# Which queue issues the first loads of an adaLN transformer block: the conditioning vector, two x blocks and a piece of w_mod

## The chip, the cores and the metric

The kernel runs on one core of a Trainium2 chip. The metric is the device time of one execution in microseconds (us), the median over several executions; lower is better. The engines of the core are named as in the profile: PE (matrix products; PEld is its loading of stationary operands), DVE (vector), ACT (scalar, activations), POOL (general), and SP, which here only issues transfers. ACT issues transfers too; a q behind a name (SPq, ACTq) marks the issuing instructions.

## The reference

One block of a transformer with adaptive layer norm, for 2048 rows of width 640, in bfloat16. The conditioning vector `c` yields six rows of modulation, which enter both layer norms and both residual additions:

```python
mod = (silu(c) @ w_mod).reshape(1, 6, 1, -1)          # w_mod: 640 x 3840
sa, ca, ga, sb, cb, gb = (mod[:, i] for i in range(6))
h = layernorm(x) * (1 + ca) + sa
x = x + ga * A(h)     # attention: 32 heads of 20, causal, window of 256, then @ wo
h = layernorm(x) * (1 + cb) + sb
x = x + gb * B(h)     # (sigmoid(h @ w_gate) * (h @ w_up)) @ w_down, inner width 1536
```

## The kernel before

The rows are worked in eight chunks of 256 rows, each two blocks of 128 rows. For every chunk the kernel normalizes and modulates x, turns it, multiplies by wqkv, turns Q and K, forms the scores, the exponentials and the products with V, multiplies by wo, and runs the gated MLP. PE's order interleaves the stages of neighbouring chunks. The order of all operations is a table, `PRIO`: each of the 2121 operations has one number, whose rank is its place and whose remainder by five is its engine (0 PE, 1 ACT, 2 DVE, 3 POOL, 4 SP). Every engine works through its own list strictly in that order. Where one engine depends on another, it waits for a semaphore; a transfer signals one of 24 semaphores in turn. Before the change, `schedule()` also ran a small model of the times, by which it chose the buffer (slot) of each tile.

The change concerns the first microseconds. What has to arrive there, in the names of the profile:

- `in_c_dram` into a corner of the buffer `oT`: the conditioning vector, 5 rows of 128 values, 1.2 KB.
- `in_A_x_dram` into `x`: the 128-row blocks of the input, 160 KB each. Block 0 goes to buffer x10, block 1 to x11.
- `in_w_mod_dram` into `wd`: the first 1280 columns of w_mod (the shift and scale of the first layer norm), in five pieces of 128 rows, 320 KB each. They lie in the buffer that later holds w_down, so the profile calls them `wd`.
- `in_A_wqkv_dram` into `wqkv`: four pieces of 400 KB (Q and K), one of 800 KB (V).

What is done with them until the first product with wqkv, engine by engine:

- PE runs matmuls without a result (L649, six, later four; L660 between the pieces), a small product that turns `c` into a column (L634), then for each piece of w_mod ten matmuls (L668, `S<-silubc,wd`), and ahead of the last piece the turning of the normalized blocks (L668, `<-ident,x`). Then the products of chunk 0 with wqkv begin (L668, `M<-wqkv,hT`).
- DVE takes the layer-norm statistics of block 0 (L776), then `c_col` (L636), the aggregate of block 0 (L778), the two steps of silu(c) that follow ACT's tanh (L638, L640), and only then the statistics of block 1 (L776, L778). POOL raises both variances to the power -1/2 (L783), DVE normalizes (L796). When PE has turned the blocks and the last piece is in, DVE copies the modulation out of PSUM (`mA`, L761), and DVE and ACT apply it (L847, L846); that gives `hT`.
- ACT issues two transfers, loads its table (L637), and computes the tanh of `c_col` (L637).

Each transfer here is issued by `dma()`, whose issuing line is L570 in the profile.

Of the kernel before, what the change touches and what calls it, by code (L numbers as in the profile page):

```python
# [22 lines left out]
SM_SCALE = 1.0 / math.sqrt(DH)  # L23
VW = 22
NDMA = 24
SWITCH = 0.095
ENGATTR = {"pe": "tensor", "act": "scalar", "dve": "vector", "pool": "gpsimd", "sp": "sync"}
ENGS = ("pe", "act", "dve", "pool", "sp")
OVERLAP = {"pe": 0.0, "act": 0.085, "dve": 0.075, "pool": 0.045, "sp": 0.0}


class Res:
# [49 lines left out]
class Prog:  # L82
# [69 lines left out]
    def schedule(self):  # L152


        free = {e: START for e in ENGS}
        bw = 0.0
        lastturn = False
        order = {e: [] for e in ENGS}
        dmacnt = [0] * NDMA
        dmalast = [None] * NDMA  # L160
        rr = 0
        pemode = 0
        portend = 0.0
        freed = {}

        def slot_time(pool, s):
            ten = pool.tenant[s]
            if ten is None:
                if not all(x.done for x in pool.init[s]):
                    return None  # L170
                return max([x.end + x.lat for x in pool.init[s]], default=0.0)
            return None if ten.left else freed[ten]

        def take(t, s):
            ten = t.pool.tenant[s]
            t.prev = list(t.pool.init[s]) if ten is None else list(ten.rel)
            t.slot = s
            t.pool.tenant[s] = t

        for o in sorted(self.ops, key=lambda x: x.prio):  # L180
            assert all(d.done for d in o.deps), o.tag
            e = ENGS[o.prio % 5]
            assert e in o.engs, (o.tag, e)
            o.eng = e
            st = max([o.tmin, free[e] + (SWITCH if e == "pe" and o.mode != pemode else 0.0)]
                     + [d.end + (0.0 if d.eng == "pe" and e == "pe" else d.lat) for d in o.deps])
            if o.isdma and e == "sp":
                st = max(st, bw - QMAX)
            for t in o.tiles:
                if t.slot is None:  # L190
                    step = 1 if t.mate is None else 2
                    best = None
                    for s in range(0, len(t.pool.tenant), step):
                        rts = [slot_time(t.pool, s + k) for k in range(step)]
                        if None not in rts and (best is None or max(rts) < best[0]):
                            best = (max(rts), s)
                    assert best is not None, (o.tag, t.name)
                    if t.mate is None:
                        take(t, best[1])
                    else:  # L200
                        take(t, best[1] + t.odd)
                        take(t.mate, best[1] + 1 - t.odd)
                for x in t.prev:
                    st = max(st, x.end + x.lat)
            if e == "dve" and o.port:
                st = max(st, free["pool"])
            elif e == "pool":
                st = max(st, portend)
            o.start = st
            if e == "pe":  # L210
                pemode = o.mout
            dur = o.dur[e]
            free[e] = st + dur - OVERLAP[e]
            if e == "dve" and o.port:
                portend = free[e]
            if o.isdma:
                turn = o.dlat > 3.0
                if e == "sp" and bw - st > 2.0:
                    free[e] += 0.35 if o.dur[e] > 1.0 else 0.1
                bw = max(st + o.dlat, bw + (MIXED if turn != lastturn and bw > st + o.dlat else 0.0)) + o.work  # L220
                lastturn = turn
                o.end = max(bw - 0.83, st + dur)
                s = rr
                rr = (rr + 1) % NDMA
                dmacnt[s] += 16
                o.key, o.val = f"d{s}", dmacnt[s]
                if dmalast[s] is not None:
                    o.deps.append(dmalast[s])
                dmalast[s] = o
            else:  # L230
                o.end = st + dur
            order[e].append(o)
            o.done = True
            for t in o.tiles:
                t.left -= 1
                if t.left == 0:
                    last = {}
                    for x in t.ops:
                        if x.isdma:
                            last[x] = x  # L240
                    for e2 in ENGS:
                        xs = [x for x in t.ops if x.eng == e2 and not x.isdma]
                        if xs:
                            last[e2] = max(xs, key=lambda x: x.start)
                    t.rel = list(last.values())
                    freed[t] = max(x.end + x.lat for x in t.rel)
        self.order = order
        self.span = max(o.end for o in self.ops)

    def emit(self):  # L250
        nc = self.nc
# [85 lines left out]
def c_pe(n):  # L337
    return max(n, 64) / 2400.0 + 0.0027


PE_EPS = 0.14
PRIO = [
# [117 lines left out]
]  # L460
TR1 = 2
NPH = 3
NPQ = 2
PQ = ()
KEEP = 3
DSAFE = 1.5
START = 0.8
PORTLAG = 0.05
MIXED = 0.55
NPB = 0  # L470
GB = ()
XT0 = 1
# [9 lines left out]
DEDGE = 0.245  # L482
FILL = 1
WSE = (("dve", "pool"), ("dve", "pool"))
QMAX = 4.5
WDT = 72.0
PAIR = 0
PAIRO = 0
# [5 lines left out]
def build(nc, A_x, A_wqkv, A_wo, B_x, B_w_gate, B_w_up, B_w_down, c, w_mod, out, S=2048):  # L494
# [50 lines left out]
    c_row = p_oT.aps[0][0:NDT, 0, 0:128]  # L545
# [19 lines left out]
    def dma(dst, src, work, reads=(), writes=(), prio=50.0, tmin=0.0, tag="dma", extra=(), nonc=False, hold=(), eng="sp", lat=0.08 + DSAFE, dur=0.5, dlat=2.24):  # L565
        def fn(e, _):
            if nonc:
                with nc.allow_non_contiguous_dma(reason="small"):
                    return e.dma_start(dst(), src())
            return e.dma_start(dst(), src())  # L570
        return A(eng, fn, dur, reads=reads, writes=writes, prio=prio, work=work, tmin=tmin, tag=tag, extra=extra, hold=hold, lat=lat, dlat=dlat)
# [23 lines left out]
    def load_x(pool, b, prio, tmin=0.0, eng="sp", extra=()):  # L595
# [2 lines left out]
            tag=f"x{b}" if pool is p_x0 or b < 2 * KEEP else f"y{b}", eng=eng, lat=(0.6, 0.9)[b] if b < 2 else 0.2 + DSAFE, extra=extra)  # L598
        return t

    dma(lambda: c_row, lambda: c.rearrange("o (t p) -> (o t) p", p=128), 0.05, writes=[R_crow], prio=-1, eng="act", lat=0.3)
    wm_src = w_mod.rearrange("(t p) f -> p t f", p=128)
    Rm = [[R(f"wm{i}_{kt}") for kt in range(NDT)] for i in range(4)]
    wm23 = hhall[:, 0:2 * NDT * D].rearrange("p (t f) -> p t f", t=NDT)
    wm_ap = [wd[:].rearrange("p a b -> p (a b)")[:, 0:6400].rearrange("p (t f) -> p t f", t=NDT),
             wu[:].rearrange("p a b -> p (a b)")[:, 0:6400].rearrange("p (t f) -> p t f", t=NDT),
             wm23[:, :, D:2 * D], wm23[:, :, 0:D]]

    def load_bulk(dst, src, Rs, work, prio, tag, extra=(), cuts=(1, 2, 3, 4, 5), **kw):
        k = 0  # L610
        for m in cuts:
            dma(lambda k=k, m=m: dst[:, k:m, :], lambda k=k, m=m: src[:, k:m, :], work * (m - k), writes=Rs[k:m],
                prio=prio + 0.01 * k, tag=tag, extra=list(extra), **kw)
            k = m
# [6 lines left out]
    x0 = {}  # L621
    keep = {}
    keep[0], keep[1] = load_x(p_x1, 0, 0), load_x(p_x1, 1, 0, eng="act", tmin=1.25)
    load_bulk(wm_ap[0], wm_src[:, :, 0:1280], Rm[0], 0.93, 0.2, "wm0", lat=0.9)
    for i in range(4):
        load_w3(320 * i, 320 * i + 320, 1.1, 0.30 + 0.005 * i, "wq" if i < 2 else "wk", lat=0.5)
    keep[2], keep[3] = load_x(p_x1, 2, 0.32), load_x(p_x1, 3, 0.33)
# [24 lines left out]
    for i in range(5):  # L652
        o = A("pe", warm, 0.85 if i < 4 else 0.43, prio=90, reads=[R_z], extra=wprev, tag="warm", writes=[R("w")])
# [302 lines left out]
    last = {"s": fills, "p": []}  # L956
# [350 lines left out]
```

## Time and profile before

| | |
|---|---|
| median of 3 runs | 325.69 us (325.58 to 326.39) |
| the profiled execution: first to last instruction | 324.3 us |
| PE busy | 317.3 us (98%) |
| PEld busy | 222.7 us (69%) |
| DVE, ACT, POOL busy | 211.8, 212.3, 187.2 us |
| granted TensorE clock | 1.000 |
| read from HBM, written | 21.30 MB, 5.25 MB |

The page gives the profiled execution's span, 324.3 us, and no time around it; the median of the timed runs is 1.4 us longer. Where PE is busy nearly all the time, the reader should not look at shares but at the few places where PE waits, and most of that waiting lies in the first 11 us. The rows of the timeline give a start, a duration, an engine with its line, and in brackets the idle time before it with what ended it.

### The profile page before, as it was taken

What the parts mean: (1) busy time and instruction counts of PE and PEld (TensorE: products, weight loads), DVE (VectorE), ACT (ScalarE), POOL (GpSimd) and SP (SyncE); (2) the same over time, 40 slices, a digit from 0 to 9 for tenths busy, and PEclk for the clock granted to TensorE, in tenths of its full rate; (3) what the DMA queues carried; (4) which work ended last, traced back from release to release, by engine and by line L of the source; (5) the groups of instructions that cost most, each with busy time, mean ns of one, the idle gap of its engine ahead of it and who ended that gap; (6) DMA issues with size and microseconds to landing.
All of it is one profiled execution on the core that took longest, in us unless ns stands there. A gap on an engine that the chain in (4) does not pass through costs nothing.

```text
span 324.3 us, 11594 instructions
## 1 busy us (share of the span) xinstructions
PE 317.3 (98%) x4872; PEld 222.7 (69%) x4873; DVE 211.8 (65%) x424; ACT 212.3 (65%) x316; POOL 187.2 (58%) x276
## 2 busy tenths in 40 slices
PE   8999999989999999999999999999999999999997
PEld 3564545446776568765776467877786788787885
DVE  5797898778687959674477475837463769264332
ACT  1899985889876687788687867786767764011120
POOL 5128869976668694847585939382939691012100
DMA  7998799989891383824405394340213032202101
GB/s 249 371 333 299 165 269 180 200 137 183 260 164 22 83 109 77 152 61 101 85 22 82 97 103 110 92 69 5 81 40 88 3 79 53 76 20 64 40 2 40
DMA packets 71694, 37.85 MB, mean 117 GB/s; under 512 B 45274, under 2 KB 70362, under 8 KB 71642
## 3 DMA queue, kind: packets, MB, share of 16 engines
q1 hardware_dynamic: 69616, 35.31, 48.3%
q10 hardware_dynamic: 2026, 1.80, 2.1%
q8 instruction: 38, 0.62, 0.8%
q14 instruction: 14, 0.11, 0.1%
HBM read 21.30 MB, written 5.25 MB: 82 GB/s over the span
## 4 chain that ended last, share of the span: by engine, by line
PE 73%; DMA 2%; SPq 2%; DVE 1%; POOL 1%; issue 0%; DVEq 0%
PE M L668 61%; PE S L669 6%; PE M L669 5%; DMA gbc<-gate 2%; SPq L803 2%; DVE wd L1192 1%; POOL x L793 0%; POOL st L788 0%; DVE hh L1211 0%; POOL E L1040 0%; DVE x L1230 0%; DVEq L310 0%
## 5 line engine op out<-in xcount | busy, mean ns | idle before, releaser
L1040 POOL TENSOR_SCALAR_AFFINE_SELECT E<-E 128x512 bf16<-128x512 bf16 (+1 forms) x176 | 142.6, 836 | 68.7 <-ACT E L1015 67.0
L1015 ACT ACTIVATE E<-S 128x512 bf16<-128x512 f32 (+2 forms) x184 | 150.9, 878 | 47.4 <-PE S L669 46.5
L668 PE MATMUL M<-wqkv,hT 128*128 128x480 bf16 (+1 forms) x340 | 73.9, 355 | 0.6 <-ACT hT L846 0.5
L668 PE MATMUL M<-h2T,wu 128*128 128x256 bf16 x480 | 68.0, 273 | 0.5 <-DVE hh L1211 0.5
L668 PE MATMUL M<-h2T,wg 128*128 128x256 bf16 x480 | 67.8, 273 | 0.0
L668 PE MATMUL M<-wd,hh 128*128 128x320 bf16 (+2 forms) x396 | 58.1, 295 | 0.0
L1209 ACT ACTIVATE sig<-M 128x512 f32<-128x512 f32 x48 | 28.9, 602 | 44.1 <-PE M L668 41.7
L1211 DVE SCALAR_TENSOR_TENSOR hh<-sig,M 128x512 bf16<-128x512 f32 x48 | 32.4, 681 | 37.1 <-ACT sig L1209 24.0
L668 PEld LDWEIGHTS M<-h2T,wu 128*128 128x128 bf16 x480 | 45.9, 98 | 8.4 <-issue 1.2
L668 PEld LDWEIGHTS M<-h2T,wg 128*128 128x128 bf16 x480 | 45.7, 98 | 7.1
L668 PEld LDWEIGHTS M<-wqkv,hT 128*128 128x128 bf16 x340 | 30.1, 98 | 27.6 <-DMA wqkv<-in_A_wqkv_dram 1.6
L668 PEld LDWEIGHTS M<-wd,hh 128*128 128x128 bf16 x396 | 36.8, 98 | 14.3 <-DVE hh L1211 0.2
L669 PEld LDWEIGHTS S<-QT,KT 20*64 20x64 bf16 (+1 forms) x1856 | 19.9, 100 | 21.3 <-ACT E L1015 12.0
L1230 DVE TENSOR_TENSOR x<-M,x 128x320 bf16<-128x320 f32 (+2 forms) x33 | 15.6, 476 | 27.2 <-PE M L668 27.2
L669 PE MATMUL S<-QT,KT 20*64 20x256 bf16 (+5 forms) x1856 | 32.1, 228 | 1.2 <-ACT E L1015 1.2
L776 DVE BATCH_NORM_STATS2 st<-x 128x6 f32<-128x320 bf16 x64 | 28.6, 477 | 2.3 <-DMA x<-in_A_x_dram 1.9
L1082 DVE STREAM_TRANSPOSE T<-M 128x512 f32<-128x512 f32 x32 | 21.5, 698 | 9.2 <-PE S L669 8.0
L668 PE MATMUL M<-wo,oT 128*128 128x320 bf16 x160 | 25.4, 299 | 0.0
L669 PE MATMUL M<-E,V 128*32 128x128 bf16 (+1 forms) x960 | 22.8, 246 | 0.8 <-ACT E L1015 0.4
L781 POOL TENSOR_SCALAR st<-st 128x2 f32<-128x2 f32 x16 | 3.7, 234 | 33.8 <-DVE st L778 33.6
L669 PEld LDWEIGHTS M<-E,V 128*32 128x32 bf16 x960 | 19.2, 97 | 5.3 <-issue 2.9
L1091 DVE STREAM_TRANSPOSE On<-Tn 128x1024 bf16<-128x1024 bf16 x16 | 19.8, 1240 | 0.3
(77 smaller groups left out, 240.2 us busy)
## 6 DMA issues: line engine op xcount, KB each, us to landing
x<-in_A_x_dram SPq DMA_DIRECT2D x23, 160.0 KB, 2.3
doc<-On SPq DMA_DIRECT2D x56, 40.0 KB
wd<-in_B_w_down_dram SPq DMA_DIRECT2D x4, 480.0 KB
wd<-in_w_mod_dram SPq DMA_DIRECT2D x5, 320.0 KB
wqkv<-in_A_wqkv_dram SPq DMA_DIRECT2D x4, 400.0 KB
wu<-in_w_mod_dram SPq DMA_DIRECT2D x5, 320.0 KB
oT<-doc SPq DMA_DIRECT2D x8, 192.0 KB, 2.5
out_dram<-x SPq DMA_DIRECT2D x9, 160.0 KB
```

Of the source, the lines that this page charges most:

```text
L668: return e.matmul(o, l, r, start=st, stop=sp, skip_group_check=True)
L669: return e.matmul(o, l, r, start=st, stop=sp, tile_position=tp, skip_group_check=True)
L776: A("dve", lambda e, g, bi=bi, j=j: e.bn_stats(v(bi * 12 + j * 6, 6), src[bi].ap[:, j * 320:(j + 1) * 320]), 0.48, reads=[src[bi].r()], wr ...
L781: A("pool", lambda e, g: e.tensor_scalar(v(28, n), var(), EPS, None, op0=ALU.add), 0.2, reads=[st.r(("m", bi)) for bi in range(n)], writes ...
L803: return e.dma_start_transpose(dst(), src())
L1015: A("act", lambda e, eng: e.activation(dst(), src(), ACT.Exp, scale=SM_SCALE), c_act(n), reads=[Sp.r()], writes=[E.r(key)], prio=3, tag=f" ...
L1040: A("pool", lambda e, eng: e.affine_select(rows(dst), rows(src), pattern=[[0, 8], [sign, n]], compare_op=ALU.is_ge, fill=0.0, base=base, c ...
L1082: A("dve", lambda e, g, h=h: e.transpose(T1.ap[:, 512 * h:512 * h + 512], X[h].ap), 0.694, reads=[X[h].r()], writes=[T1.r(h)], prio=3.5, t ...
L1091: A("dve", lambda e, g: e.transpose(On.ap[:], Tn.ap[:]), 1.22, reads=[Tn.r()], writes=[On.r()], prio=4, tag=f"tr2_{a}")
L1209: A("act", lambda e, g, pg=pg, sg=sg: e.activation(sg.ap[:], pg.ap[:], ACT.Tanh, scale=0.5), c_act(512), reads=[pg.r()], writes=[sg.r()], ...
L1211: A("dve", lambda e, g, pu=pu, sg=sg, f0=f0: e.scalar_tensor_tensor(out=hh.ap[:, f0:f0 + 2, :], in0=sg.ap[:].rearrange("p (a b) -> p a b", ...
L1230: A("dve", lambda e, g, ps=ps, bi=bi, c0=c0, n=n: e.tensor_tensor(x1[bi].ap[:, c0:c0 + n], ps.ap[:, 0:n], x1[bi].ap[:, c0:c0 + n], op=ALU. ...
```

## The change

Three of the first four transfers change places, and one changes its engine with another:

- The conditioning vector was ACT's first transfer; it is now SP's first, ahead of x block 0.
- The first of the five pieces of w_mod was SP's second transfer; it is now ACT's first, ahead of x block 1.
- The other four pieces stay on SP, behind x block 0.

On ACT, from the start of its list, before:

```order
L322 UNCONDITIONAL_BRANCH
L570 DMA oT0<-in_c_dram 5x128
L570 DMA x11<-in_A_x_dram 128x640
L637 ACT_TABLE_LOAD
L637 ACTIVATE cth<-c_col 128x5
```

and after, where the line numbers are smaller since the file became shorter:

```order
L271 UNCONDITIONAL_BRANCH
L536 DMA wd<-in_w_mod_dram 128x1280
L536 DMA x11<-in_A_x_dram 128x640
L603 ACT_TABLE_LOAD
L603 ACTIVATE cth<-c_col 128x5
```

A transfer of 320 KB stands where one of 1.2 KB stood; x block 1 (x11) and the table load keep their places behind it.

On SP, from the start of its list, before:

```order
L322 UNCONDITIONAL_BRANCH
L570 DMA x10<-in_A_x_dram 128x640
L570 DMA wd<-in_w_mod_dram 128x1280 x5
L570 DMA wqkv<-in_A_wqkv_dram 128x5x320 x2
L570 DMA x12<-in_A_x_dram 128x640
```

and after:

```order
L271 UNCONDITIONAL_BRANCH
L536 DMA oT0<-in_c_dram 5x128
L536 DMA x10<-in_A_x_dram 128x640
L536 DMA wd<-in_w_mod_dram 128x1280 x4
L536 DMA wqkv<-in_A_wqkv_dram 128x5x320 x2
```

x block 0 (x10) is second instead of first, and one piece of w_mod has left the queue. On PE, DVE and POOL, and behind these rows on ACT and SP, every row and every buffer number is the same before and after, so the four transfers are all that moves.

The diff also takes the model of the times out of `schedule()` and puts a fixed table of slots, `SLOTS`, in the place of its choice. Cut to its core:

```diff
@@ PRIO: the ranks of the first operations
-    23, 28, 258, 8, 43, 33, 958, 18, 1448, 38, 3, 507, 513, 72, 67, 48, 53, 58, 76, 84, 101, 99, 144, 149, 154, 159,
+    28, 33, 258, 13, 48, 38, 958, 23, 1448, 43, 8, 507, 513, 77, 72, 53, 58, 63, 4, 89, 101, 81, 144, 149, 154, 159,
...
@@ def schedule(self):
-                    for s in range(0, len(t.pool.tenant), step):
-                        rts = [slot_time(t.pool, s + k) for k in range(step)]
...
+                    s = SLOTS[tiles[t]] if SLOTS else 0
...
@@ the loads
-    dma(lambda: c_row, lambda: c.rearrange("o (t p) -> (o t) p", p=128), 0.05, writes=[R_crow], prio=-1, eng="act", lat=0.3)
+    dma(lambda: c_row, lambda: c.rearrange("o (t p) -> (o t) p", p=128), 0.05, writes=[R_crow], prio=-1, eng=("sp", "act"), lat=0.3)
...
-    load_bulk(wm_ap[0], wm_src[:, :, 0:1280], Rm[0], 0.93, 0.2, "wm0", lat=0.9)
+    load_bulk(wm_ap[0], wm_src[:, :, 0:1280], Rm[0], 0.93, 0.2, "wm0", lat=0.9, eng=("act", "sp"))
```

In `PRIO` the numbers 76, 84, 101, 99 (the vector on ACT, block 0 on SP, block 1 on ACT, the first piece on SP) became 4, 89, 101, 81 (the vector on SP with rank 0, block 0 on SP, block 1 on ACT, the first piece on ACT).

More of the change, by code (lines that the diff above doesn't have):

```diff
@@ L25 @@
 NDMA = 24
-SWITCH = 0.095
 ENGATTR = {"pe": "tensor", "act": "scalar", "dve": "vector", "pool": "gpsimd", "sp": "sync"}
 ENGS = ("pe", "act", "dve", "pool", "sp")
-OVERLAP = {"pe": 0.0, "act": 0.085, "dve": 0.075, "pool": 0.045, "sp": 0.0}
 class Res:
@@ L152, in schedule @@
     def schedule(self):
-        free = {e: START for e in ENGS}
-        bw = 0.0
-        lastturn = False
         order = {e: [] for e in ENGS}
@@ L161, in schedule, with number @@
         rr = 0
[L162 to L178, printed above, removed]
+        tiles = {}
+        def number(t):
+            if t is not None and t not in tiles:
+                tiles[t] = len(tiles)
+                number(t.mate)
+        for o in self.ops:
+            for t in o.tiles:
+                number(t)
         for o in sorted(self.ops, key=lambda x: x.prio):
@@ L184, in schedule @@
             o.eng = e
[L185 to L188, printed above, removed]
             for t in o.tiles:
                 if t.slot is None:
-                    step = 1 if t.mate is None else 2
-                    best = None
-                    for s in range(0, len(t.pool.tenant), step):
-                        rts = [slot_time(t.pool, s + k) for k in range(step)]
[L195 to L215, printed above, removed]
-            if o.isdma:
[L217 to L223, printed above, removed]
-                rr = (rr + 1) % NDMA
[L225 to L231, printed above, removed]
+                    s = SLOTS[tiles[t]] if SLOTS else 0
@@ new lines, in schedule @@
+                    ten = t.pool.tenant[s]
+                    assert ten is not None or all(x.done for x in t.pool.init[s]), (o.tag, t.name)
+                    assert ten is None or ten.left == 0, (o.tag, t.name)
+                    t.prev = list(t.pool.init[s]) if ten is None else list(ten.rel)
+                    t.slot = s
+                    t.pool.tenant[s] = t
+            if o.isdma:
+                dmacnt[rr] += 16
+                o.key, o.val = f"d{rr}", dmacnt[rr]
+                if dmalast[rr] is not None:
+                    o.deps.append(dmalast[rr])
+                dmalast[rr] = o
+                rr = (rr + 1) % NDMA
@@ L237, in schedule @@
                     last = {}
[L238 to L244, printed above, removed]
+                    for x in sorted(t.ops, key=lambda x: x.prio):
+                        last[x if x.isdma else x.eng] = x
                     t.rel = list(last.values())
-                    freed[t] = max(x.end + x.lat for x in t.rel)
         self.order = order
-        self.span = max(o.end for o in self.ops)
     def emit(self):
@@ L338, in c_pe @@
     return max(n, 64) / 2400.0 + 0.0027
-PE_EPS = 0.14
 PRIO = [
[4 rows of a table removed]
[4 rows of a table added]
     367, 362, 412, 422, 391, 417, 396, 380, 400, 406, 620, 655, 672, 515, 521, 820, 827, 465, 470, 476, 530, 535,
@@ L460 @@
 ]
+SLOTS = [
[20 rows of a table added]
+]
 TR1 = 2
@@ L466 @@
 DSAFE = 1.5
-START = 0.8
-PORTLAG = 0.05
-MIXED = 0.55
 NPB = 0
@@ L484 @@
 WSE = (("dve", "pool"), ("dve", "pool"))
-QMAX = 4.5
 WDT = 72.0
```

26 rows, old and new, of tables (PRIO, SLOTS) are left out of this document.

## The prediction

> **What bounds the kernel now.** First the page: its span and PE's share say whether a start can matter at all.
>
> ```profile
> span 324.3 us, 11594 instructions
> PE 317.3 (98%) x4872; PEld 222.7 (69%) x4873; DVE 211.8 (65%) x424; ACT 212.3 (65%) x316; POOL 187.2 (58%) x276
> ```
>
> PE is without work for 7.0 us of 324.3. What comes late before PE's long run begins has little room to be made up later. A difference of 0.3% is 0.98 us, about what a measurement of this kernel can tell from no change; so the question is whether the four moved transfers shift PE by a microsecond. Second, the timeline of the issuing queues:
>
> ```profile
> 0.79 0.39 SPq L570 DMA_DIRECT2D x<-in_A_x_dram  x1
> 1.25 2.31 SPq L570 DMA_DIRECT2D wd<-in_w_mod_dram  x5
> 3.60 1.16 SPq L570 DMA_DIRECT2D wqkv<-in_A_wqkv_dram  x2
> 7.01 2.18 SPq L570 DMA_DIRECT2D x<-in_A_x_dram  x1
> 0.79 0.57 ACTq L570 DMA_DIRECT2D oT<-in_c_dram  x1
> 1.40 0.37 ACTq L570 DMA_DIRECT2D x<-in_A_x_dram  x1
> ```
>
> An issue costs 0.37 to 0.57 us at first; by 7.01 SP is held 2.18 us for one block: the transfers, not the issuing, set the pace by then. Third, the timelines of DVE, ACT and POOL, in which the reader follows one chain:
>
> ```profile
> 3.08 0.89 DVE L776 BATCH_NORM_STATS2 st<-x 128x6 f32<-128x320 bf16 x2 [1.42 <-DMA x<-in_A_x_dram]
> 4.20 0.17 DVE L636 TENSOR_SCALAR c_col<-M 128x5 bf16<-128x5 f32 x1 [0.23 <-PE M L634]
> 4.64 0.17 DVE L638 SCALAR_TENSOR_TENSOR siluc<-cth,c_col 128x5 bf16<-128x5 f32 x1 [0.16 <-ACT cth L637]
> 4.84 0.49 DVE L640 COPY silubc<-siluc 128x320 bf16<-128x320 bf16 x1
> 5.24 0.88 DVE L776 BATCH_NORM_STATS2 st<-x 128x6 f32<-128x320 bf16 x2
> 6.16 0.21 DVE L778 BATCH_NORM_AGGREGATE st<-st 128x2 f32<-128x12 f32 x1
> 7.58 0.80 DVE L796 TENSOR_SCALAR x<-x,st 128x640 bf16<-128x640 bf16 x2 [1.22 <-POOL st L783]
> 9.50 0.17 DVE L761 COPY mA<-S 128x10 f32<-128x10 f32 x1
> ...
> 4.40 0.21 ACT L637 ACTIVATE cth<-c_col 128x5 f32<-128x5 bf16 x1 [1.32 <-DVE c_col L636]
> ...
> 6.82 0.73 POOL L783 TENSOR_TENSOR st<-st,mhalf 128x2 f32<-128x2 f32 x1
> ```
>
> Block 0 lands at 3.08 (its statistics wait for the transfer until then), they end at 3.97, and DVE has 0.23 us to spare before `c_col` at 4.20, which waits for PE. From there each step starts when the one before it ends: tanh 4.40, silu 4.64, its copy 4.84, statistics of block 1 at 5.24 (no wait for its transfer, so it had landed), aggregate 6.16, power 6.82, normalization 7.58 to 8.38. Last, PE:
>
> ```profile
> 1.31 2.74 PE L649 MATMUL S<-E 128*128 128x512 bf16 x6 [1.31 <-DVE E L644]
> 3.98 0.18 PE L634 MATMUL M<-ident,oT 5*128 5x5 bf16 x1
> 4.33 1.91 PE L649 MATMUL S<-E 128*128 128x512 bf16 x4
> 6.04 0.58 PE L668 MATMUL S<-silubc,wd 128*128 128x64 bf16 x10
> 7.23 0.35 PEld L668 LDWEIGHTS S<-silubc,wd 128*128 128x128 bf16 x10 [0.20 <-DMA wd<-in_w_mod_dram]
> 8.10 0.35 PEld L668 LDWEIGHTS S<-silubc,wd 128*128 128x128 bf16 x10 [0.49 <-DMA wd<-in_w_mod_dram]
> 8.44 0.45 PEld L668 LDWEIGHTS M<-ident,x 128*128 128x128 bf16 x8
> 10.33 0.13 PEld L668 LDWEIGHTS M<-wqkv,hT 128*128 128x128 bf16 x2 [0.93 <-DMA wqkv<-in_A_wqkv_dram]
> 11.16 1.20 PEld L668 LDWEIGHTS M<-wqkv,hT 128*128 128x128 bf16 x10 [0.21 <-DMA wqkv<-in_A_wqkv_dram]
> 13.28 0.54 PEld L668 LDWEIGHTS M<-wqkv,hT 128*128 128x128 bf16 x5 [0.18 <-DMA wqkv<-in_A_wqkv_dram]
> 14.76 0.52 PEld L668 LDWEIGHTS M<-wqkv,hT 128*128 128x128 bf16 x5 [0.31 <-DMA wqkv<-in_A_wqkv_dram]
> ...
> 10.36 2.33 PE L668 MATMUL M<-wqkv,hT 128*128 128x320 bf16 x15 [0.47 <-ACT hT L846]
> 13.00 1.15 PE L668 MATMUL M<-wqkv,hT 128*128 128x320 bf16 x7
> 14.21 1.41 PE L668 MATMUL M<-wqkv,hT 128*128 128x320 bf16 x8
> ```
>
> The turning of the blocks follows the normalization at 8.44, the last piece's product stands behind it in PE's list, `mA` is copied at 9.50, and the first product with wqkv waits for `hT` until 10.36. So two strands run neck and neck: the chain from `c_col` to 10.36, and the stream of loads, which holds PE again at 11.16, 13.28 and 14.76.
>
> **The change part by part.** *The first piece on ACT at 0.79 instead of SP at 1.25.* It comes up to 0.46 us earlier, but nobody waits for it: its product starts at about 6.04, behind PE's four matmuls of 4.33, while the waits for `wd` are those for the third and fourth pieces. Worth nothing by itself.
>
> *The vector on SP.* Its issue stands at 0.79 as before. PE takes it up at 3.98, behind matmuls without a result; that is 2.6 us after its issue ended, against 1.9 us for block 0 (1.18 to 3.08). Nothing, so long as it isn't held up by the piece for over 0.7 us; and a delay would be covered by the next item.
>
> *The later loads on SP.* In front of them stand the vector (0.57 us to issue, if SP needs what ACT needs) and block 0, in place of block 0 and one more piece (2.31 / 5 = 0.46): 0.11 us later. The bytes ahead of the first wqkv piece are the same. Since SP is held by the transfers from then on, I put the stream at no change, with bounds from 0.46 us earlier (the piece's gain) to 0.11 us later.
>
> *ACT's table load* stood behind 0.57 + 0.37 us of issues, and now stands behind 0.46 + 0.37; its cover is the 1.32 us that ACT waits before 4.40. Nothing.
>
> *Block 0 behind the vector and beside the piece.* This is the term that counts. Its issue moves from 0.79 to between 1.24 (0.39 us for the vector) and 1.42 (0.57), plus the same gap of 0.06. When does it land? The stretches of 0.5 us, last columns the share of the transfer engines and GB/s:
>
> ```profile
> 1.50:2.00 0.50, 0.50 (x2) 0.15 (x1) 0.16 (x1) 0.20 (x1) 0.37 (x3) 1.00 0.26 27
> 2.00:2.50 0.50, 0.50 (x2) 0.15 (x1) 0.00 (x0) 0.50 (x1) 0.50 (x3) 1.00 0.85 252
> 2.50:3.00 0.50, 0.50 (x3) 0.16 (x2) 0.00 (x0) 0.50 (x1) 0.50 (x7) 1.00 0.98 218
> 3.00:3.50 0.50, 0.50 (x3) 0.14 (x1) 0.42 (x2) 0.08 (x1) 0.50 (x3) 1.00 0.67 248
> 3.50:4.00 0.50, 0.50 (x3) 0.02 (x1) 0.47 (x2) 0.00 (x0) 0.50 (x2) 1.00 1.04 387
> 4.00:4.50 0.50, 0.50 (x4) 0.35 (x4) 0.28 (x2) 0.10 (x1) 0.45 (x1) 1.00 1.07 348
> ```
>
> Summed, 140 kB have moved by 2.5, 373 by 3.5, 566 by 4.0, 740 by 4.5. Block 0 (164 kB) was through at about 2.61 and landed at 3.08: a lag of 0.47. If the same stream now carries the piece first (328 kB) and then block 0 alone, block 0 is through at 492 kB, which is 3.81, and lands at 4.28. If block 1, issued beside it, shares the engines, both are through at 656 kB, 4.26, and land at 4.73. I take 4.5, the middle, because the two blocks are issued almost together. The bounds: as quick from its issue as now (2.29 us), it lands at 3.53; as slow as block 1 now can have been (1.40 to at most 5.24, 3.84 us), at 5.26.
>
> [...]
>
> Behind block 0 on DVE waits `c_col`, and so everything down to 10.36. Landing at 4.5 is 1.42 later than 3.08; less DVE's 0.23 to spare, `c_col` and the chain are 1.19 late. The first product with silu(c) has some 0.6 us to spare (copy ends at 5.33, product at 6.04) and PE still catches up with the pieces by 8.44, so this adds nothing of its own. The first product with wqkv starts at 11.55.
>
> How much does the stream give back? Where PE is unhindered:
>
> ```profile
> 295.71 6.55 PE L668 MATMUL M<-wd,hh 128*128 128x320 bf16 x47
> ...
> PEld M L668 <- DMA wqkv<-in_A_wqkv_dram: 1.6, 4, 0.9
> ```
>
> The last of 47 matmuls runs 0.30, so 46 steps take 6.25: 0.136 us each. By that, the groups of 15, 7 and 8 lost (2.03 - 1.90) + (0.85 - 0.82) + (1.11 - 0.95) = 0.32 us, of which some 0.07 goes to the second wait for `hT`, which moves along. So 0.25 us of waiting for loads vanishes when PE comes later. The list of waits has no other wait of PE for wqkv than the four seen by 14.76, and ACT's exponentials, PE's next partner, are fed by the same chain; I see nothing behind that a late start meets as cover.
>
> Sum: 1.42 - 0.23 - 0.25 = +0.94 us. The profiled span goes from 324.3 to 325.2. The median of the timed runs, 325.69, lies 1.4 above that span for what is around it, so it goes to 326.6.
>
> **The rivals.** *Block 0 isn't late (not slower).* If the piece doesn't hold up block 0, it lands at 3.53, `c_col` is 0.45 - 0.23 = 0.22 late, and the 0.25 us of waits for loads cover that; with the stream early by up to 0.46, those waits go instead. That is 0.0 to -0.25: 325.4 to 325.7. It decides where block 0 lands by 3.56 (3.08 + 0.23 + 0.25). For it: the share of 0.67 at 3.0 to 3.5, room in the engines. Against it: block 0 needed 2.29 us when it was alone at the start.
>
> *The stream was the bound (faster).* If all later loads come 0.46 us earlier and the chain counts for less than I read, 0.46 us is the most: 325.2, still not a difference that can be told. A gain of 1 us has no row for it.
>
> *PE's slow pace returns.* The four matmuls from 4.33 run until 6.04, 0.43 us for 512 columns, against 0.136 for 320 late in the kernel (0.217 for 512): half the pace. Should the longer pauses before 8.44 and 11.55 bring that back for as long as it lasted at first (1.3 to 6.0, 4.7 us), 2.3 us come on top: 328.9. [...] The granted clock of 1.00 in all rows above, the slow ones too, can't show it.
>
> *Nothing moves.* The transfers interleave so that only the order of issues changes: 325.7.
>
> **How the numbers follow.** Chances: block 0 late 0.73, with the landing anywhere from 4.0 to 5.26 and so +0.45 to +1.7 us (326.1 to 327.4); of this 0.45 lies above 0.98 us, as 4.5 sits right at the edge, the landing that block 1 shows is far above it, and the slack of 0.25 is the least sure of the terms. Block 0 not late 0.12; slow pace 0.06; stream or something unseen that gains over 1 us 0.06; nothing moves 0.03. So slower by over 0.3%: 0.45 + 0.06 = 0.51; faster 0.06; within 0.43. The range runs from 325.3, the lower end of the second case with a little of the runs' spread, to 327.6, the upper end of the first with the same; outside lie the slow pace and the unseen gain.
>
> **What would show it.** Right: the statistics of block 0 start at 4.3 to 4.7 instead of 3.08; `c_col` has no wait for PE any more and starts at about 5.4; the first product with wqkv starts at 11.3 to 11.8; PE's waits for wqkv at 11.16 to 14.76 are gone or small; the products that start at 14.21 come about 0.9 later, and so does the end. Wrong: block 0 lands before 3.6; or the chain is late and the end isn't, which would mean slack behind 16 us that I overlooked; or the end moves by more than the first product does.

## The result, and the profile after

The changed kernel takes 326.19 us (median of 19 runs, 325.97 to 327.47), the kernel before 325.69 us (325.22 to 326.66, 19 runs). The ratio is 1.0017, 95% interval 1.001 to 1.0025: 0.5 us slower. That is less than the 0.3% from which the prediction counts a time as slower, but the interval excludes no change.

The page of the changed kernel: the span is 0.5 us longer than the 324.3 of before, PE's busy time 0.9 us less. Of the 0.9, 0.82 us is four matmuls without a result early on (1.91 us in the profile of before, 1.09 here); the second profile of the changed kernel has them at 1.91 again, so this goes with the execution.

```profile
span 324.8 us, 11594 instructions
PE 316.4 (97%) x4872; PEld 222.6 (69%) x4873; DVE 211.4 (65%) x424; ACT 212.2 (65%) x316; POOL 187.2 (58%) x276
```

The timeline of the issuing queues (start, duration, queue, line, what is loaded):

```profile
0.79 0.38 SPq L536 DMA_DIRECT2D oT<-in_c_dram  x1
0.79 0.39 ACTq L536 DMA_DIRECT2D wd<-in_w_mod_dram  x1
1.21 0.48 ACTq L536 DMA_DIRECT2D x<-in_A_x_dram  x1
1.24 0.36 SPq L536 DMA_DIRECT2D x<-in_A_x_dram  x1
1.65 1.84 SPq L536 DMA_DIRECT2D wd<-in_w_mod_dram  x4
3.53 1.12 SPq L536 DMA_DIRECT2D wqkv<-in_A_wqkv_dram  x2
```

The vector takes SP 0.38 us to issue, where it took ACT 0.57. So block 0 is issued at 1.24, the lower of the two bounds, and the first wqkv load at 3.53, against 3.60 before. The stretches of 0.5 us (last columns: clock, share of the transfer engines, GB/s):

```profile
1.50:2.00 0.50, 0.50 (x2) 0.15 (x1) 0.16 (x1) 0.28 (x1) 0.38 (x3) 1.00 0.45 48
2.00:2.50 0.50, 0.50 (x2) 0.15 (x1) 0.00 (x0) 0.50 (x1) 0.50 (x3) 1.00 0.75 200
2.50:3.00 0.50, 0.50 (x3) 0.16 (x2) 0.00 (x0) 0.50 (x1) 0.50 (x7) 1.00 0.87 341
3.00:3.50 0.50, 0.50 (x3) 0.14 (x1) 0.00 (x0) 0.00 (x1) 0.50 (x3) 1.00 1.00 359
3.50:4.00 0.50, 0.50 (x3) 0.03 (x1) 0.00 (x0) 0.00 (x0) 0.50 (x2) 1.00 1.10 405
```

By 4.0 us 677 kB have moved (half of 48 + 200 + 341 + 359 + 405), where it was 566 kB; in the second profiles of both kernels (below) it is 628 and 554. The gain comes between 2.5 and 4.0 us; by 2.5 the changed kernel, with large transfers at the head of both queues, has moved less (124 kB against 140). Now the timeline of DVE and ACT, row for row as before:

```profile
4.14 0.89 DVE L742 BATCH_NORM_STATS2 st<-x 128x6 f32<-128x320 bf16 x2 [2.48 <-DMA x<-in_A_x_dram]
4.94 0.15 DVE L602 TENSOR_SCALAR c_col<-M 128x5 bf16<-128x5 f32 x1
5.13 0.21 ACT L603 ACTIVATE cth<-c_col 128x5 f32<-128x5 bf16 x1 [2.12 <-DVE c_col L602]
5.57 0.49 DVE L606 COPY silubc<-siluc 128x320 bf16<-128x320 bf16 x1
5.97 0.88 DVE L742 BATCH_NORM_STATS2 st<-x 128x6 f32<-128x320 bf16 x2
8.31 0.80 DVE L762 TENSOR_SCALAR x<-x,st 128x640 bf16<-128x640 bf16 x2 [1.22 <-POOL st L749]
```

Block 0 lands at 4.14 instead of 3.08. `c_col` has lost its wait for PE and stands 0.74 later; tanh, copy, block 1's statistics and the normalization are 0.73 to 0.74 later each. The chain moved as one piece. On PE:

```profile
6.20 0.45 PE L634 MATMUL S<-silubc,wd 128*128 128x64 bf16 x10 [0.78 <-DVE silubc L606]
7.93 0.35 PEld L634 LDWEIGHTS S<-silubc,wd 128*128 128x128 bf16 x10 [0.36 <-DMA wd<-in_w_mod_dram]
9.17 0.62 PE L634 MATMUL M<-ident,x 128*128 128x128 bf16 x8 [0.77 <-DVE x L762]
11.06 0.13 PEld L634 LDWEIGHTS M<-wqkv,hT 128*128 128x128 bf16 x2 [0.93 <-issue]
11.09 2.28 PE L634 MATMUL M<-wqkv,hT 128*128 128x320 bf16 x15 [0.47 <-ACT hT L812]
13.68 1.15 PE L634 MATMUL M<-wqkv,hT 128*128 128x320 bf16 x7
14.89 1.25 PE L634 MATMUL M<-wqkv,hT 128*128 128x320 bf16 x8
16.07 0.40 PE L635 MATMUL S<-QT,KT 20*128 20x256 bf16 x8
```

PE now waits 0.77 us for the normalized blocks ahead of their turning, a wait that did not stand there before. The first product with wqkv is 0.73 later. No row waits for wqkv any more, and the three groups of products are 2.28, 1.15 and 1.25 us long, together 0.21 shorter. The first scores, which the timeline of before has in this row,

```profile
15.55 0.40 PE L669 MATMUL S<-QT,KT 20*128 20x256 bf16 x8
```

are 0.52 later. Behind 16 us nothing is given back: the products of the exponentials with V at 38.23 (`M<-E,V`) stand at 38.77 (+0.54), the scores at 64.13 at 64.60 (+0.47), and the span ends 0.5 later. So the whole difference is made in the first 16 us.

### The profile page after: what moved, and what is told of

Same layout as the page of the kernel before. It is cut to its first block, busy times and chain, and to the rows that moved or that the text cites. A ratio compares the mean times of both kernels' runs of the same rounds, so it can differ in the third digit from the quotient of the medians.

```text
span 324.8 us, 11594 instructions
## 1 busy us (share of the span) xinstructions
PE 316.4 (97%) x4872; PEld 222.6 (69%) x4873; DVE 211.4 (65%) x424; ACT 212.2 (65%) x316; POOL 187.2 (58%) x276
## 4 chain that ended last, share of the span: by engine, by line
PE 72%; DMA 2%; SPq 2%; DVE 1%; POOL 1%; issue 0%; DVEq 0%
PE M L634 61%; PE S L635 6%; PE M L635 5%; DMA gbc<-gate 2%; SPq L769 2%; DVE wd L1158 0%; POOL x L759 0%; POOL st L754 0%; DVE hh L1177 0%; POOL E L1006 0%; DVE x L1196 0%; DVEq L259 0%
```

## The experiments

Each experiment changes a few ranks in `PRIO` of the changed kernel, behind the table; the remainder by five is the engine, and a larger number a later place. Operation 18 is the vector, 19 and 20 are blocks 0 and 1, 21 to 25 the five pieces of w_mod. In the first ones Theory A is the prediction's reading, that block 0's landing moves the chain; in the last two it is what the runs before them had made of it. The table has the start of the steps in each profiled execution (block 0's landing is the start of the statistics that wait for it; only with silu first do they wait for DVE instead, and the landing is at or before that start) and the timed runs; the kernel before, timed beside them on the same chip, had 325.65 us (first four rows of experiments), 325.61 (next four) and 325.47 (last two).

| kernel | block 0 | c_col | normalization | first product | first scores | median us | ratio to before, 95% |
|---|---|---|---|---|---|---|---|
| before | 3.08 | 4.20 | 7.58 | 10.36 | 15.55 | 325.69 | |
| after | 4.14 | 4.94 | 8.31 | 11.09 | 16.07 | 326.19 | 1.0017 (1.0010 to 1.0025) |
| vector alone | 3.54 | 4.34 | 7.70 | 11.23 | 16.52 | 326.76 | 1.0032 (1.0021 to 1.0043) |
| piece alone | 3.11 | 4.20 | 9.60 | 12.62 | 18.41 | 328.21 | 1.0076 (1.0053 to 1.0098) |
| block 0 first | 3.95 | 4.76 | 8.16 | 10.95 | 15.93 | 326.27 | 1.0019 (1.0009 to 1.0030) |
| block 0 later | 5.54 | 6.34 | 9.70 | 12.48 | 17.46 | 327.93 | 1.0069 (1.0053 to 1.0085) |
| before again | 3.35 | 4.20 | 7.58 | 10.48 | 15.76 | 325.64 | 0.9998 (0.9987 to 1.0008) |
| after again | 4.26 | 5.06 | 8.42 | 11.20 | 16.18 | 326.21 | 1.0017 (1.0005 to 1.0029) |
| statistics first | 4.33 | 5.14 | 7.67 | 10.88 | 15.86 | 326.15 | 1.0026 (1.0002 to 1.0050) |
| silu first | by 4.38 | 3.34 | 7.71 | 10.88 | 16.15 | 325.97 | 1.0003 (0.9993 to 1.0014) |
| last piece on ACT | 3.17 | 4.20 | 7.57 | 11.85 | 16.83 | 326.77 | 1.0035 (1.0020 to 1.0051) |
| that, statistics first | 3.21 | 4.20 | 7.28 | 11.47 | 16.45 | 326.95 | 1.0039 (1.0020 to 1.0058) |

**The vector alone.** The first piece goes back to SP, behind block 0; ACT issues only block 1.

```diff
+PRIO[21] = 99
```

> Half of the change: the vector first on SP, ahead of x block 0, but all five pieces of w_mod on SP behind block 0; ACT issues x block 1 first. Theory A (block 0 lands late, DVE takes its statistics ahead of c_col, and the chain to the first product with wqkv is late by the landing minus 3.40 us): block 0 is issued at 1.24 with no piece ahead of it, only block 1 beside it; it lands at 3.5 to 3.8, the first product comes at 10.5 to 10.8, the span is 324.3 to 324.6. Rival B (the piece ahead of block 1 on ACT costs, whatever block 0 does): as before, 324.3. Rival C (the vector on SP costs): as the changed kernel, 324.8.

Block 0 landed as expected (3.54), 0.60 earlier than after, and the normalization starts 0.61 earlier; but the expected first product between 10.5 and 10.8 did not come, and the time is, if anything, longer than after's (the intervals of the two ratios overlap at 1.0021 to 1.0025; the first scores at 16.52, against 16.07 and 16.18, point the same way). Three of its stretches and a row of PE's weight loads:

```profile
3.00:3.50 0.50, 0.50 (x3) 0.14 (x1) 0.00 (x0) 0.00 (x0) 0.50 (x3) 1.00 0.91 115
3.50:4.00 0.50, 0.50 (x3) 0.02 (x1) 0.46 (x2) 0.00 (x0) 0.50 (x2) 1.00 0.75 148
4.00:4.50 0.50, 0.50 (x5) 0.33 (x5) 0.50 (x4) 0.00 (x0) 0.44 (x1) 1.00 0.69 215
...
9.01 0.35 PEld L635 LDWEIGHTS S<-silubc,wd 128*128 128x128 bf16 x10 [1.27 <-DMA wd<-in_w_mod_dram]
```

With the vector and the two blocks ahead of all pieces, the stream has a hole from 3.0 to 4.5 us: 115, 148 and 215 GB/s, where the changed kernel has 359 and 405 in the first two of these stretches, and all four profiles with its transfers have 351 to 412 in the three. The transfer engines are not idle in the hole (share 0.91, 0.75, 0.69); why they move so little is not shown. The fourth piece holds PE until 9.01, though the normalization is nearly in time. So the stream ends last here, and with the first piece on ACT, the only difference from the changed kernel, the hole is not there.

**The piece alone.** The vector goes back to ACT's head; the first piece stands behind it and block 1 third.

```diff
+PRIO[18] = 1
```

> The other half: the vector stays first on ACT, the first piece of w_mod follows it on ACT ahead of x block 1, and SP issues x block 0 first and then the four other pieces. Theory A: block 0 lands at 3.1 to 3.3 as before, c_col stays at 4.20, the first product at 10.36, span 324.2 to 324.4. Rival B: the whole cost, 324.8. Rival C: no cost, 324.3. With the run before, A and C differ by where the cost sits: A finds it in neither half alone, or a part of it in the first.

Block 0 and `c_col` came as expected (3.11, 4.20), as in the kernel before; the first product and the time did not, since block 1 became the one that lands last:

```profile
7.25 0.89 DVE L743 BATCH_NORM_STATS2 st<-x 128x6 f32<-128x320 bf16 x2 [1.93 <-DMA x<-in_A_x_dram]
10.46 0.62 PE L635 MATMUL M<-ident,x 128*128 128x128 bf16 x8 [2.40 <-DVE x L763]
11.02 0.70 PE L635 MATMUL S<-silubc,wd 128*128 128x64 bf16 x10
12.62 3.09 PE L635 MATMUL M<-wqkv,hT 128*128 128x320 bf16 x15
...
PEclk9799999999999999999999999999999999999999
...
10.50:11.00 0.50, 0.50 (x10) 0.50 (x11) 0.22 (x1) 0.11 (x1) 0.00 (x0) 1.00 1.09 367
11.10:14.40 3.30, 3.03 (x20) 1.57 (x19) 3.04 (x12) 2.62 (x8) 0.00 (x0) 0.50 1.11 369
14.50:17.00 2.50, 2.50 (x24) 1.73 (x23) 1.85 (x8) 1.77 (x5) 1.29 (x3) 1.00 1.10 369
```

Block 1, issued at 1.79 behind a piece on its own queue, lands at 7.25; before, it was there by 5.24. PE waits 2.40 us for the normalized blocks, and behind that pause the pace is lower: ten matmuls with the last piece take 0.70 us instead of 0.46, fifteen products 3.09 instead of 2.28, and the granted clock's second slice is 0.7. The last three rows are stretches, with the clock in the third column from the end: it is 1.00 up to 11.0 us, 0.50 from 11.1 to 14.4, and 1.00 again from 14.5. (In steps of 0.1 us the 0.50 holds from 11.07 to 14.48, 3.4 us.) This is the prediction's rival of the slow pace, in another kernel than the one it was written for. It is not the whole loss: the two executions at a granted clock of 1.000 took 327.03 and 327.29 us, the four at 0.995 took 328.20 to 329.29, so some 1.5 of the 2.6 us over the kernel before came without it.

**Block 0 first.** On SP block 0 stands ahead of the vector; ACT as in the changed kernel.

```diff
+PRIO[18] = 94
```

> The changed kernel with one pair of transfers exchanged: SP issues x block 0 first and the vector second; the piece stays first on ACT. Theory A: block 0 goes out at the same moment as the piece, lands at 3.1 to 3.6, c_col at 4.2 to 4.4, first product 10.36 to 10.56, span 324.2 to 324.5: most of the 0.46 us comes back. Rival B: 324.8. Rival C in its form that the vector must not come later: it is issued at 1.25 behind block 0 and beside the piece; if it lands after PE asks for it at 3.98, the product L600 comes late and c_col waits for PE instead.

The landing expected at 3.1 to 3.6 did not come. Block 0 is issued at 0.79, as in the kernel before, and lands 0.87 later than there:

```profile
3.95 0.89 DVE L743 BATCH_NORM_STATS2 st<-x 128x6 f32<-128x320 bf16 x2 [2.29 <-DMA x<-in_A_x_dram]
4.45 0.18 PE L601 MATMUL M<-ident,oT 5*128 5x5 bf16 x1 [0.41 <-DMA oT<-in_c_dram]
```

So the larger part of the 1.06 us is not the place in SP's queue but the piece that now runs beside block 0 on ACT's queue. The place adds 0.19 here (3.95 to 4.14), no more than landings differ between executions, and 0.46 with no piece beside it (3.54 with the vector alone). The piece costs block 0 nothing when it is issued at 1.39, behind the vector (3.11 with the piece alone). The vector, second on SP, is late in its turn, and PE waits 0.41 us for it; but `c_col` still starts 0.81 behind block 0's landing, as in the changed kernel (0.80), so block 0 stays the later of the two, and `c_col` gains the 0.18 that block 0 gains. The first scores are 0.14 earlier, the time the same within its interval.

**Block 0 later.** One of SP's pieces goes ahead of block 0.

```diff
+PRIO[22] = 84
```

> The dose: the changed kernel with x block 0 one place further back on SP, behind the vector and the second piece of w_mod. The bytes ahead of wqkv and every other order are the same. Theory A: block 0 lands 0.7 to 1.0 us later than in the changed kernel, at 4.8 to 5.1; c_col, the first product and the end move by the same 0.7 to 1.0, since the waits for loads that gave back 0.2 are used up: span 325.5 to 325.8. Rivals B and C, and a theory that the stream of loads sets the end: 324.8.

The dose was larger than expected (1.40 us instead of 0.7 to 1.0), and the answer has slope one:

```profile
5.54 0.89 DVE L743 BATCH_NORM_STATS2 st<-x 128x6 f32<-128x320 bf16 x2 [3.88 <-DMA x<-in_A_x_dram]
6.34 0.15 DVE L603 TENSOR_SCALAR c_col<-M 128x5 bf16<-128x5 f32 x1
12.48 2.28 PE L635 MATMUL M<-wqkv,hT 128*128 128x320 bf16 x15 [0.47 <-ACT hT L813]
```

Against the changed kernel: landing +1.40, `c_col` +1.40, first product +1.39, first scores +1.39, median +1.7 (+1.35 for the three of its six executions at a granted clock of 1.000). So beyond DVE's time to spare, a later block 0 goes through to the first scores in full.

**Both kernels again,** unchanged, for the spread from one profiled execution to another.

> The kernel before, unchanged, profiled again beside the others. The first product with wqkv at 10.36, within 0.1, if the start repeats from run to run. In the profile on record PE waits 0.51 us at 86.54 behind DVE; in the four experiments so far that wait is gone and everything after it comes 0.6 to 0.7 us earlier. If the wait belongs to the run and not to the kernel, it can be absent here too and the span then is 323.6 to 323.8.

> The changed kernel, unchanged, profiled again on the same chip. Theory A: block 0's statistics again start at 4.0 to 4.3, the first product at 11.0 to 11.2, so 0.6 to 0.8 later than in the kernel before, and 0.4 to 0.6 later from 16 us on. If the wait at 86 us belongs to the run, it is absent or present in both, and the spans differ by 0.4 to 0.6.

```profile
3.35 0.89 DVE L776 BATCH_NORM_STATS2 st<-x 128x6 f32<-128x320 bf16 x2 [1.69 <-DMA x<-in_A_x_dram]
4.20 0.17 DVE L636 TENSOR_SCALAR c_col<-M 128x5 bf16<-128x5 f32 x1
...
4.26 0.89 DVE L742 BATCH_NORM_STATS2 st<-x 128x6 f32<-128x320 bf16 x2 [2.60 <-DMA x<-in_A_x_dram]
5.06 0.15 DVE L602 TENSOR_SCALAR c_col<-M 128x5 bf16<-128x5 f32 x1
```

The first two rows are the kernel before, the other two the changed one. In this execution of the kernel before block 0 lands 0.27 later than in the first, with `c_col` still at 4.20: DVE's time to spare, seen directly. The landings of one kernel differ by 0.1 to 0.3 us from one profile to the other, the spans by 0.4 to 0.5: they are 323.8 and 324.4 here. Half a microsecond of the first two spans is a wait of PE that both had (0.51 us for `hh`, at 86.54 before and 87.01 after) and that neither has here. A single span therefore tells no difference of half a microsecond; the timed runs and the first scores do, +0.57 and +0.42 in this pair.

**Statistics first.** `c_col` and then both blocks' statistics and aggregates come ahead of the two steps of silu on DVE; the transfers as in the changed kernel.

```diff
+PRIO[42] = 122
+PRIO[72] = 127
+PRIO[73] = 132
+PRIO[74] = 137
+PRIO[75] = 142
```

> The changed kernel's four transfers as they are; on DVE alone the statistics of block 1 and its aggregate now stand ahead of the two silu steps. Theory A (DVE's queue, busy without a gap from block 0's landing on, is what makes the chain late): the normalization starts at 7.5 to 7.7 instead of 8.31, the first product with silu(c) at 6.8 to 6.9 and the four pieces then run to 8.7, so the blocks are turned at about 8.7 and the first product with wqkv comes at 10.5 to 10.7: 0.4 to 0.6 of the 0.73 comes back. If the loads themselves made the start late: 11.1.

```profile
7.15 0.45 PE L639 MATMUL S<-silubc,wd 128*128 128x64 bf16 x10 [1.59 <-DVE silubc L611]
7.67 0.80 DVE L767 TENSOR_SCALAR x<-x,st 128x640 bf16<-128x640 bf16 x2 [0.66 <-POOL st L754]
10.88 2.28 PE L639 MATMUL M<-wqkv,hT 128*128 128x320 bf16 x15 [0.47 <-ACT hT L817]
```

In the profile the normalization is back to 7.67, nearly as before and as expected, with block 0 as late as after; but the products with the pieces now start at 7.15, not at 6.8 to 6.9, and end last, the first product comes at 10.88 and not by 10.7, and of the 0.75 us that the normalization won against after again (8.42) the first scores keep 0.32. The timed runs spread from 325.60 to 330.03: six of the twelve lie at 325.60 to 325.81, the profiled one among them, and six at 326.49 and above; their interval holds the changed kernel's 1.0017 and nearly reaches no change, so they settle nothing.

**Silu first.** The small product that makes the column, `c_col`, tanh and both silu steps come ahead of block 0's statistics.

```diff
+PRIO[41] = 115
+PRIO[49] = 120
+PRIO[42] = 117
+PRIO[43] = 126
+PRIO[44] = 127
+PRIO[45] = 132
+PRIO[71] = 137
+PRIO[70] = 142
+PRIO[72] = 147
```

> The changed kernel's four transfers as they are; PE takes the vector's product two matmuls earlier, and DVE does c_col, silu and its copy ahead of both blocks' statistics, while it waits for block 0 anyway. Theory A: silu's copy ends at 4.3 to 4.5, the statistics of both blocks run from then without a gap, the normalization starts at 7.1 to 7.4, the blocks are turned behind the fourth piece at 8.4, and the first product with wqkv comes at 10.2 to 10.4: as before the change or 0.1 earlier, with the first piece's earlier landing kept. The time is that of the kernel before, or 0.1 to 0.2 us less. If the loads themselves made the start late: 11.1 and 0.5 us more than before.

```profile
7.71 0.80 DVE L771 TENSOR_SCALAR x<-x,st 128x640 bf16<-128x640 bf16 x2 [1.21 <-POOL st L758]
7.89 0.35 PEld L643 LDWEIGHTS S<-silubc,wd 128*128 128x128 bf16 x10 [1.10 <-DMA wd<-in_w_mod_dram]
8.67 0.35 PEld L643 LDWEIGHTS S<-silubc,wd 128*128 128x128 bf16 x10 [0.40 <-DMA wd<-in_w_mod_dram]
```

With `c_col` at 3.34 it no longer stands behind block 0. The statistics of block 0 start at 4.38, right behind silu's copy and without a wait for the transfer, so block 0 had landed by then; the normalization is back at 7.71, where 7.1 to 7.4 was expected. PE then waits for the pieces (1.10 and 0.40 us), so the stream is what ends last in this profile: the first product, expected by 10.4, comes at 10.88, 0.32 ahead of after again, the first scores only 0.03 ahead. The stream itself was later here than in the changed kernel, though the transfers are the same: the third piece's products start at 7.89, against 7.21 and 7.37 without a wait in the two profiles of the changed kernel, and by 7.0 us 1487 kB have moved, against 1597 and 1579 there and 1672 with the statistics first. Whether the earlier order or the single execution makes it late is not shown. The ratio, 1.0003 (0.9993 to 1.0014), shows neither a loss nor a gain against the kernel before, though its interval overlaps the changed kernel's and the medians lie 0.36 us apart (325.97 and 325.61). What the run shows is the queue on DVE: with nothing of silu behind block 0's statistics, their start at 4.38 leads to a normalization at 7.71, where after again, with a start at 4.26, has 8.42.

**The last piece on ACT.** A try for something better than both: vector and block 1 on ACT and block 0 at SP's head as before, and the fifth piece as ACT's third transfer.

```diff
+PRIO[18] = 1
+PRIO[21] = 139
+PRIO[25] = 106
```

> A new arrangement with both early blocks as in the kernel before: the vector and then block 1 on ACT, block 0 first on SP, and as ACT's third transfer the last of the five pieces, which PE needs only at about 8.9 us. Theory A (the start is a race of four arrivals, and the kernel before was balanced within 0.2 to 0.4 us): block 0's statistics at 3.1 to 3.4, c_col at 4.20, normalization at 7.6, first product with wqkv at 10.3 to 10.5; SP reaches the wqkv loads one issue (0.46 us) sooner, so PE's waits for wqkv behind 11 us shrink by 0.2 to 0.3: 325.3 to 325.6. Rival: the piece on ACT takes its share of the transfer engines from the pieces on SP, and the fourth piece or block 1 comes later than now: normalization or turning 0.3 to 1 us late, 326.0 to 326.6.

```profile
7.57 0.80 DVE L765 TENSOR_SCALAR x<-x,st 128x640 bf16<-128x640 bf16 x2 [1.21 <-POOL st L752]
7.93 0.35 PEld L637 LDWEIGHTS S<-silubc,wd 128*128 128x128 bf16 x10 [1.26 <-DMA wd<-in_w_mod_dram]
9.63 0.35 PEld L637 LDWEIGHTS S<-silubc,wd 128*128 128x128 bf16 x10 [0.51 <-DMA wd<-in_w_mod_dram]
11.85 2.28 PE L637 MATMUL M<-wqkv,hT 128*128 128x320 bf16 x15 [0.47 <-ACT hT L815]
```

The rival came, larger than put: the chain is as before (7.57), but PE waits for the second, third and fourth piece, and the first product is 1.49 us late. That the piece needed last takes its share of the transfer engines from those needed first, as the rival has it, fits; no view parts the bytes of one transfer from those of another.

**That, with the statistics first** (the three lines of the run before it and the five of "statistics first").

> The same four transfers, and in DVE's list both blocks' statistics and aggregates ahead of the two silu steps. Theory A: if block 1 has landed by 4.5, normalization starts at 6.8 to 7.2 and the turning of the blocks then waits only for the fourth piece; the first product with wqkv comes at 9.9 to 10.3 and the time is 325.0 to 325.5. Rival (block 1 lands just ahead of 5.2, where the kernel before takes it up): the statistics wait, silu comes late with them, and it is 325.7 to 326.2.

```profile
4.93 0.89 DVE L750 BATCH_NORM_STATS2 st<-x 128x6 f32<-128x320 bf16 x2 [0.46 <-DMA x<-in_A_x_dram]
```

Block 1 lands at 4.93, later than the 4.5 that the gain needed, and the stream is late as in the run before it: the first product comes at 11.47, the time is 326.95 us, over both expectations. None of the arrangements that were run is measurably better than the kernel before.

## Why the prediction was right, and where its sizes were off

The forecast was 326.6 us (325.3 to 327.6), block 0 late; measured were 326.19. The sum and its measured terms:

| term | put | measured |
|---|---|---|
| block 0 lands later by | 1.42 | 1.06 |
| DVE's time to spare ahead of `c_col` | -0.23 | -0.32 |
| PE's waits for wqkv that vanish | -0.25 | -0.21 |
| sum | +0.94 | +0.53 |

- *Block 0 behind the vector and beside the piece.* The mechanism was right, its size too large: this is the term that was mis-sized. The landing was put at 4.5, and it came at 4.14 (4.26 in the second profile), ahead even of the 4.28 of "piece first". Two of its parts failed. The vector's issue was bounded by 0.39 and 0.57 and took 0.38. And the bytes were read off the stream of the kernel before, which reached 492 kB at 3.81; the changed one has 474 kB by 3.5 and so reaches 492 at 3.54, which with the lag of 0.47 is 4.01, an estimate. By the same rates the shared case, 656 kB, is through at 3.95 and lands at 4.42. The two landings lie between, which fits the two cases, taken at the wrong rate; no run parts the one from the other. The direction followed from the mechanism; that 326.19 lies within the forecast, at half of the +0.94, owes something to the width of its range.
- *Where the delay comes from.* The prediction named both causes, "behind the vector and beside the piece", and did not part them. With block 0 first in the queue, 0.87 us of delay remain (0.60 against the later landing of before again, 3.35), and the piece at ACT's head is what differs; the vector alone ahead of it makes 0.46 (0.19). Each delays block 0 by itself, the piece more, and the two do not add up. Why a piece on the other queue makes a block that is issued first land 0.87 us late, no run here shows.
- *DVE's 0.23 to spare* was 0.32: `c_col` starts 0.80 us after the first of the statistics, 0.09 before their rows end. The second profile of the kernel before shows the spare directly, with block 0 0.27 later and `c_col` unmoved.
- *The chain behind it* went as put: `c_col` to first product is 6.16 before and 6.15 after. From normalization to first product it is 2.78 or 2.79 in before, after, after again, and the runs with block 0 first and later. Where it is longer, a piece (2.90 in before again, 3.53 with the vector alone), the slow pace (3.02 with the piece alone) or late products with silu(c) (3.21 with the statistics first) came in.
- *The stream gives back* 0.21 of the 0.25, and nothing later, as put.
- *The first piece on ACT, "worth nothing by itself",* was wrong as a statement on the change's halves, though the sum hardly felt it. Without the piece the stream has a hole, and the median is 0.57 us longer (326.76 against 326.19, with intervals that overlap a little). The stream at "no change" held for the whole change; in the half without the piece it does not, so it was right by luck more than by its reason.
- *The signs.* Right: `c_col` without its wait for PE, the waits for wqkv gone. Just outside: block 0 at 4.14 (4.3 to 4.7 was said), `c_col` at 4.94 (about 5.4), first product at 11.09 (11.3 to 11.8); the last products 0.68 later, where 0.9 was said.
- *The chances.* Slower by over 0.3% had 0.51, since 4.5 sat at the edge. The result lies on the other side of that edge, within 0.3% but with an interval that excludes no change.
- *The rivals.* "Block 0 isn't late" and "nothing moves" are excluded by the landing. "The stream was the bound" failed for this change, but the stream ended last in the profiles of two kernels with a shorter chain (vector alone; silu first, whose stream was itself late). "PE's slow pace returns" didn't happen here, where the longest pauses were 0.78 and 0.77 us, and did in the kernel with one of 2.40. Its chance of 0.06 was the author's judgement; no run shows that the pause is the cause.

What the runs put in the place of "two strands neck and neck" is a race of four arrivals: block 0, block 1, the vector, and the stream of pieces. The kernel before has three of them within a few tenths: block 0 (0.32 us to spare), block 1 (needed at 5.24; with the last piece on ACT and the statistics first it lands at 4.93), and the stream, whose fourth piece holds PE until 8.11, just ahead of the turning at 8.44. Of the vector it shows only that it had landed by 3.98, when PE took it up behind matmuls without a result. Rearranging made one or another the last: block 0 in the changed kernel and with block 0 first or later, block 1 with the piece alone, the stream with the vector alone and with the last piece on ACT; the vector was the last in none, though PE waited for it with block 0 first. Shown by the landings and waits above; not shown is why block 1 with the piece alone needs 5.46 us from issue to landing.

## What to carry to other kernels

In the first microseconds here the rate is still rising (48 to 405 GB/s from 1.5 to 4.0 us), and a transfer is late by what runs beside it as well as by its place in its own queue: block 0 landed 0.87 us later with a piece issued at the same moment on the other queue, 0.46 later behind the vector, 1.06 later with both, and another 1.40 later with one of SP's pieces ahead of it too. So moving one is costed by all that run beside it as well as by its place, and by the rate after the change, not the rate before. When the order is changed, name for each early consumer which arrival it waits for last, and how far the next one is behind; where they are within a few tenths of a microsecond, as here, moving one can make another the last: no move that was run gained. A change with two halves should be tried in halves: here the piece alone was worse than the whole, and the vector alone probably was.

## What the runs showed of the hardware that was not expected

- *The slow pace came back after a pause of 2.40 us.* The row with the 3.09 us above shows it, against 2.28 for the same fifteen products in the changed kernel. The granted clock, which stands at 1.00 in all rows of the first slow pace, does show this one: 0.50 from 11.07 to 14.48 us, 3.4 us in all. It sets in 0.6 us behind the pause, amid matmuls. At half the pace 3.4 us cost 1.7, an estimate from this profile; the prediction's 2.3 rested on a spell of 4.7. Among the timed executions a mean granted clock of 0.995, instead of 1.000 or 0.999, is listed for 4 of 6 with the piece alone, 3 of 6 with block 0 later, 2 of 12 with the statistics first, 2 of 12 with the last piece on ACT and 3 of 12 with that and the statistics first; for none of the other kernels. Their medians are 0.6 to 2.9 us above those of the same kernel's executions at 1.000, four of the five below the 2.3 that the prediction put on this rival. In four of these five kernels the profile shows a single pause of PE of 1.49 to 2.40 us before the first product; in the fifth, the last piece on ACT, it shows only shorter ones in a row (0.75 at most). That the pauses cause it in those executions is not shown: only the piece alone was profiled in one.
- *The first lifting of the slow pace isn't fixed in time.* The four matmuls from 4.33 took 1.91 us in the profiled kernel before and 1.83 in its repeat, 1.09 in the changed kernel and 1.91 in its repeat. What sets the moment is not shown.
- *The same small transfer takes 0.57 to 0.58 us to issue on ACT and 0.35 to 0.39 on SP,* in every run; the large ones take 0.38 to 0.40 as ACT's first. No run shows why.
